# Decay in place, a one-partition gate, halved block 0, accumulated sums and a new instruction order in a linear-attention and expert kernel

## The chip, the cores and the metric

One core of one Trainium2 chip. The metric is device time of one execution in microseconds (us), as a median over several executions. A profile is one execution under the hardware profiler; its span (first to last instruction) is some 1.65 us shorter than the time of the same execution. Executions come in a fast and a slow state; ratios compare fast executions only, while medians are over all executions. All "wait" figures are idle time of an engine just before an instruction, put down to whatever released it.

## The reference

Four sequences of 768 tokens, 8 heads of 48. First a linear attention with a decaying state, then for each sequence one expert out of eight, chosen from the mean of the attention's output.

```python
for t in range(S):                                   # attention, per head
    cur = einsum('bhd,bhe->bhde', u * k_t, v_t)
    y[:, :, t] = einsum('bhd,bhde->bhe', r_t, state + cur)
    state = w * state + einsum('bhd,bhe->bhde', k_t, v_t)
x = y.transpose(0, 2, 1, 3).reshape(B, S, 384)
logits = x.mean(axis=1) @ w_gate                     # 8 experts
e_idx = argmax(logits, axis=1); gate_w = softmax(logits)[e_idx]
out[b] = gate_w[b] * (relu(x[b] @ w1[e]) @ w2[e])    # w1 384x1024, w2 1024x384
```

## The kernel before

A sequence is three blocks of 256 tokens, 12 blocks in all (block g, sequence b = g // 3). For each block k and r are scaled by powers of the decay, turned on TensorE (PE), multiplied to scores, masked on VectorE (DVE), and multiplied with v; a state in PSUM carries over. The expert's weights can only be fetched when the mean is known: gate (PE), choice (DVE), then GpSimd (POOL) reads the index and issues the transfers. The expert phase (mm1: `hp`, relu: `ht`, mm2: `op`, eviction: `ob`, store) of one sequence is interleaved with the attention of the next.

Every operation is a step with the engines that may do it; a long text gives the order. Each engine executes its steps in that order and waits for what a step needs, so an instruction that waits holds up all behind it on its engine. `b0` to `b2` are three PSUM banks that steps take and free.

```python
ORDER = """...
POOL vt 3; POOL r 5; POOL weights 0; ACT exp 0; fill 3 b0; PE at 4 0; ...
... DVE st 1 0; ...; PE carry 1; PE s 1 0; ...
SP store 1 1; SP store 1 0; SP store 1 2; ..."""

def carried(g):            # puts the decayed state back into PSUM, by a product with the identity
    nc.tensor.matmul(out=s_ps[b][:, 0 : 2 * D * NP], lhsT=ident,
                     rhs=carry[b]..., start=True, stop=False, ...)

def state_out(g, o):       # o = 1: decayed, for the next block; o = 0: within the block
    nc.vector.tensor_mul(st, s_ps[b]..., wcmask if o else bmask...)
    if o:
        carry[b] = st
        ...

def pool_mms(g):           # sums over tokens: 6 one-column matmuls for each block
    ...
def gate(b):               # logits on all 128 partitions: the stationary operand is broadcast
    for ct in range(NCT):
        nc.tensor.matmul(out=lgp, lhsT=pools[b][:, ct : ct + 1].to_broadcast([128, 128]), rhs=wg[:, ct, :], ...)

def weights(b):            # w1 as two tiles and two transfers of 384 KB, then w2
    ev = nc.gpsimd.value_load(idx8[0:1, 0:1], ...)
    for fh in range(2):
        t = wpool.tile([128, NCT, HF], BF16, tag=f"w1_{fh}", ...)
        nc.gpsimd.dma_start(out=t, in_=moe_w1[ds(ev, 1)]...[:, :, HF * fh : HF * fh + HF])
        w1s[b, fh] = t
    ...
def store(b, gi, cs):      # two transfers for one block of output
    for c in range(2):
        nc.sync.dma_start(out=dst[c][:, cs, :], in_=obs[b, gi][64 * c : 64 * c + 64, cs, :])
```

Of the kernel before, what the change touches and what calls it, by code (L numbers as in the profile page):

```python
# [19 lines left out]
DVE k 0 0; DVE r 0 0; ACT late; fill 1 b0; PE t 0 0 b0; DVE k 0 1; DVE r 0 1; J k 0; J r 0  # L20
POOL r 1; fill 2 b1; PE t 0 1 b1; ACT kr 0 1; ACT v 0; DVE kr 0 0; fill 6 b2; PE at 0 0; DVE k 1
DVE prod 0 0 b0; DVE prod 0 1 b1; DVE gt 0 0; PE t 1 0 b2; ACT kr 1 0; PE s 0 0; DVE st 0 1
PE bonus 0; PE t 1 1 b0; PE at 0 1; PE y 0 1 0; PE s 0 1; PE inter 0 1; ACT kr 1 1
DVE prod 1 0 b2; DVE gt 0 1; DVE prod 1 1 b0; POOL k 2; POOL r 2; DVE tcol 0; J vt 0; SP load 4
SP load 5; SP load 6; fill 2 b1; PE at 1 0; PE bonus 1; DVE tcol 1; DVE st 1 0; ACT v 1
POOL vt 1; DVE gt 1 0; PE t 2 1 b1; PE y 0 1 1; PE t 2 0 b2; PE carry 1; PE s 1 0; PE y 0 0 0
PE vt_y 0; PE at 1 1; DVE st 1 1; POOL k 3; POOL r 3; ACT kr 2 1; ACT kr 2 0; ACT xn 0 1
DVE gt 1 1; DVE prod 2 0 b2; DVE prod 2 1 b1; PE y 0 0 1; PE y 1 1 0; PE s 1 1; ACT xn 0 0
PE y 1 0 0; PE inter 1 0; PE at 2 0; DVE gt 2 0; PE y 1 0 1; PE inter 1 1; PE bonus 2
PE t 3 1 b0; PE at 2 1; PE turn 0 b2; DVE tcol 2; DVE st 2 0; POOL v 2; POOL vt 2; POOL k 4  # L30
POOL r 4; DVE gt 2 1; PE t 3 0 b1; PE vt_y 1; PE pool 0; PE carry 2; PE y 1 1 1; PE s 2 0
ACT v 3; ACT kr 3 1; ACT xn 1 0; ACT xn 1 1; DVE kr 3 0; DVE prod 3 1 b0; DVE st 2 1
DVE prod 3 0 b1; PE y 2 0 1; PE y 2 1 0; PE at 3 0; PE turn 1 b0; PE bonus 3; PE inter 2 1
PE y 2 0 0; PE y 2 1 1; PE vt_y 2; DVE gt 3 0; PE at 3 1; ACT v 4; ACT xt 0 b2; ACT xn 2 1
DVE tcol 3; DVE xt 1 b0; DVE gt 3 1; PE inter 2 0; ACT xn 2 0; PE t 4 1 b1; PE pool 1; PE pool 2
DVE gate_sums 0; PE t 4 0 b2; PE gate 0; ACT kr 4 1; ACT kr 4 0; DVE k 5; DVE choose 0
POOL vt 3; POOL r 5; POOL weights 0; ACT exp 0; fill 3 b0; PE at 4 0; DVE prod 4 0 b2
DVE prod 4 1 b1; DVE gt 4 0; POOL v 5; PE turn 2 b0; PE t 5 0 b2; ACT xt 2 b0; ACT kr 5 0
PE s 3 0; PE t 5 1 b1; ACT kr 5 1; DVE st 3 1; PE at 4 1; PE bonus 4; PE s 3 1; PE vt_y 3
PE inter 3 1; DVE gt 4 1; DVE st 4 0; DVE tcol 4; PE at 5 0; ACT xn 3 0; ACT xn 3 1  # L40
DVE prod 5 0 b2; DVE prod 5 1 b1; PE inter 4 0; PE carry 4; PE s 4 0; PE bonus 5
PE mm1 0 2 0 b0; PE mm1 0 3 0 b2; ACT relu 0 2 0 b0; PE mm1 0 2 1 b1; ACT relu 0 3 0 b2
ACT relu 0 2 1 b1; POOL k 6; POOL vt 4; DVE gt 5 0; DVE r 6; DVE tcol 5; PE mm1 0 0 0 b0
PE t 6 1 b2; PE t 6 0 b1; DVE st 4 1; DVE gw 0; DVE kr 6 1; DVE prod 6 1 b2; PE s 4 1; PE vt_y 4
PE at 5 1; DVE st 5 0; ACT relu 0 0 0 b0; ACT kr 6 0; DVE prod 6 0 b1; PE turn 3 b0
PE mm1 0 3 1 b2; ACT xt 3 b0; DVE xn 4 0; PE carry 5; PE mm1 0 6 0 b1; PE inter 4 1
PE mm1 0 4 0 b0; ACT relu 0 3 1 b2; DVE relu 0 6 0 b1; ACT relu 0 4 0 b0; PE inter 5 0
PE mm1 0 1 1 b2; ACT relu 0 1 1 b2; DVE gt 5 1; DVE xn 4 1; PE mm1 0 0 1 b1; PE mm1 0 5 1 b0
PE mm1 0 1 0 b2; ACT relu 0 0 1 b1; ACT relu 0 5 1 b0; PE s 5 0; DVE st 5 1; PE at 6 0
PE mm1 0 6 1 b1; DVE relu 0 1 0 b2; DVE gt 6 0; SP fence; SP load 7; SP load 8; SP load 9  # L50
PE mm1 0 7 1 b0; PE mm1 0 5 0 b2; DVE relu 0 7 1 b0; DVE r 7; ACT relu 0 6 1 b1
ACT relu 0 5 0 b2; POOL vt 5; POOL k 7; POOL r 8; PE mm1 0 4 1 b1; PE inter 5 1; PE s 5 1
PE at 6 1; PE vt_y 5; ACT v 6; ACT relu 0 4 1 b1; POOL k 9; DVE xn 5 1; PE mm1 0 7 0 b2
PE t 7 0 b0; PE pool 4; PE bonus 6; PE pool 3; PE mm2 0 5 0 b1; ACT relu 0 7 0 b2; DVE xn 5 0
DVE gt 6 1; PE pool 5; DVE gate_sums 1; PE mm2 0 5 1; DVE k 8; ACT v 7; ACT kr 7 0; PE gate 1
DVE choose 1; DVE prod 7 0 b0; PE mm2 0 1 0 b2; PE mm2 0 1 1; DVE tcol 6; ACT gated 0 5 b1
DVE vt 6; ACT gated 0 1 b2; PE t 7 1 b1; PE mm2 0 4 0 b0; PE mm2 0 4 1; PE t 8 0 b2; DVE kr 7 1
DVE prod 7 1 b1; ACT exp 1; ACT gated 0 4 b0; ACT kr 8 0; DVE r 9; PE s 6 0; PE at 7 0
PE turn 5 b1; ACT xt 5 b1; PE mm2 0 0 0 b0; PE mm2 0 0 1; DVE gt 7 0; DVE prod 8 0 b2
POOL weights 1; DVE gated 0 0 b0; PE bonus 7; PE t 9 1 b1; PE t 9 0 b2; PE t 8 1 b0; ACT v 8  # L60
ACT kr 8 1; DVE st 6 1; PE s 6 1; PE at 7 1; PE vt_y 6; ACT kr 9 0; ACT xn 6 0; DVE kr 9 1
DVE prod 9 1 b1; DVE tcol 7; DVE prod 8 1 b0; DVE st 7 0; DVE prod 9 0 b2; DVE gt 7 1; POOL vt 7
PE mm2 0 3 0 b1; PE mm2 0 2 0 b0; PE mm2 0 2 1; PE carry 7; PE inter 7 0; PE inter 6 1
PE mm2 0 3 1; PE turn 4 b2; DVE xt 4 b2; DVE gated 0 2 b0; ACT xn 6 1; PE pool 6
ACT gated 0 3 b1; PE s 7 0; PE at 8 0; DVE st 7 1; PE mm1 1 0 1 b1; PE mm1 1 5 1 b2
ACT relu 1 0 1 b1; ACT relu 1 5 1 b2; PE mm1 1 0 0 b0; ACT relu 1 0 0 b0; PE inter 7 1
PE bonus 8; PE mm1 1 6 1 b1; PE mm1 1 2 0 b2; DVE tcol 8; DVE gt 8 0; DVE gw 1
DVE relu 1 2 0 b2; DVE relu 1 6 1 b1; PE mm1 1 1 0 b0; PE s 7 1; PE vt_y 7; ACT xn 7 1
ACT relu 1 1 0 b0; ACT xn 7 0; PE at 8 1; PE mm1 1 4 0 b2; SP store 0 1; SP load 10; SP load 11
SP store 0 0; SP store 0 2; DVE st 8 0; DVE relu 1 4 0 b2; PE mm1 1 3 1 b1; DVE gt 8 1  # L70
ACT relu 1 3 1 b1; PE mm1 1 5 0 b0; ACT relu 1 5 0 b0; PE pool 7; PE inter 8 0; PE mm1 1 7 1 b2
PE mm1 1 2 1 b1; PE mm1 1 6 0 b0; ACT relu 1 6 0 b0; ACT relu 1 2 1 b1; POOL k 10; POOL vt 8
DVE r 10; POOL v 9; PE carry 8; PE s 8 0; PE at 9 0; DVE st 8 1; PE t 10 1 b0; PE inter 8 1
PE mm1 1 1 1 b1; PE s 8 1; PE vt_y 8; ACT v 10; ACT relu 1 1 1 b1; ACT relu 1 7 1 b2; DVE gt 9 0
DVE kr 10 1; DVE prod 10 1 b0; PE at 9 1; ACT xn 8 1; PE bonus 9; PE mm1 1 7 0 b1
DVE relu 1 7 0 b1; PE turn 6 b2; ACT xn 8 0; PE mm1 1 3 0 b0; PE pool 8; ACT xt 6 b2
PE mm1 1 4 1 b1; ACT relu 1 3 0 b0; ACT relu 1 4 1 b1; PE turn 8 b2; ACT xt 8 b2; POOL k 11
DVE gate_sums 2; PE gate 2; DVE gt 9 1; DVE choose 2; ACT exp 2; DVE gw 2; DVE tcol 9
PE t 10 0 b0; PE mm2 1 5 0 b1; PE mm2 1 5 1; DVE kr 10 0; DVE prod 10 0 b0; DVE vt 9
PE mm2 1 2 0 b2; PE mm2 1 2 1; DVE gated 1 5 b1; DVE gated 1 2 b2; PE at 10 0; PE s 9 0  # L80
PE mm2 1 0 0 b0; PE mm2 1 1 0 b1; PE mm2 1 1 1; ACT gated 1 1 b1; PE mm2 1 0 1; PE turn 7 b2
ACT gated 1 0 b0; ACT xt 7 b2; POOL weights 2; POOL r 11; PE t 11 0 b1; DVE gt 10 0; DVE st 9 1
PE s 9 1; PE vt_y 9; PE at 10 1; DVE kr 11 0; DVE st 10 0; PE mm1 2 3 1 b0; PE inter 9 1
DVE prod 11 0 b1; ACT xn 9 0; ACT relu 2 3 1 b0; DVE xn 9 1; PE t 11 1 b2; PE bonus 10
DVE tcol 10; PE mm1 2 0 1 b1; DVE gt 10 1; ACT relu 2 0 1 b1; PE pool 9; PE mm1 2 3 0 b0
PE inter 10 0; PE mm2 1 4 0 b1; PE mm2 1 4 1; PE carry 10; DVE relu 2 3 0 b0; ACT kr 11 1
PE at 11 0; PE s 10 0; DVE prod 11 1 b2; DVE v 11; PE mm1 2 2 1 b0; PE mm1 2 6 1 b2
ACT relu 2 6 1 b2; ACT relu 2 2 1 b0; ACT gated 1 4 b1; DVE st 10 1; DVE gt 11 0; POOL vt 10
PE bonus 11; PE s 10 1; PE vt_y 10; PE at 11 1; PE mm1 2 2 0 b2; DVE xn 10 0; ACT relu 2 2 0 b2
PE mm1 2 1 1 b0; PE mm1 2 1 0 b1; ACT relu 2 1 0 b1; ACT relu 2 1 1 b0; PE inter 10 1  # L90
DVE tcol 11; DVE st 11 0; PE mm2 1 3 0 b2; PE inter 11 0; POOL vt 11; DVE xn 10 1; DVE gt 11 1
PE mm1 2 7 0 b1; PE mm2 1 3 1; PE mm1 2 0 0 b0; PE carry 11; DVE relu 2 0 0 b0; ACT gated 1 3 b2
PE s 11 0; DVE st 11 1; PE turn 9 b2; PE mm1 2 5 0 b0; ACT relu 2 5 0 b0; ACT xt 9 b2
DVE relu 2 7 0 b1; PE s 11 1; PE vt_y 11; DVE xn 11 0; PE inter 11 1; PE mm1 2 4 0 b1
DVE xn 11 1; PE mm1 2 7 1 b0; ACT relu 2 7 1 b0; PE pool 10; PE pool 11; PE mm1 2 4 1 b2
DVE gate_sums 3; PE mm1 2 6 0 b0; PE gate 3; DVE choose 3; ACT relu 2 4 1 b2; ACT relu 2 6 0 b0
# [19 lines left out]
def kernel(  # L116
# [250 lines left out]
    def transpose_by_dma(g, i):  # L367

        if g not in krs:
            kr_tile(g)  # L370
# [173 lines left out]
    def state_out(g, o):  # L544
        b, gi = divmod(g, NB)
        if o == 1 and gi == NB - 1:
            return
# [378 lines left out]
```

## Time and profile before

| | before |
|---|---|
| time, median of 3 | 137.65 us |
| profiled execution | 141.46 us, span 139.8 |
| first expert matmul, half clock after it (us) | 38.87; 39.3 to 42.7 |
| last matmul to end of span (us) | 134.52 to 139.8 |

The slices, the windows and the chain of waits stand in the prediction. Two views are added. The first is the table of PE's waits of the kernel before (what waited and for what; total, times, longest): in the whole run there is one wait of weight.

```profile
PE hp L669 <- DMA w<-in_moe_w_dram: 2.0, 1, 2.0
PE fill L213 <- DVE zero L185: 1.3, 1, 1.3
PE twp L351 <- POOL rp L333: 0.7, 2, 0.5
```

The second is DVE's timeline of the kernel before, from the start to the choice of the first expert (start, duration, engine, line, operation, and in brackets the idle time before it).

```profile
9.05 2.57 DVE L333 TENSOR_TENSOR kp<-k,dk 128x768 bf16<-128x768 f32 x1
...
13.34 0.54 DVE L549 TENSOR_TENSOR st<-s,bmask 128x384 bf16<-128x384 f32 x1
...
28.78 0.18 DVE L607 TENSOR_REDUCE pooled<-s 128x3 f32<-128x18 f32 x1
28.87 1.03 DVE L333 TENSOR_TENSOR kp<-k,dk 128x768 bf16<-128x768 f32 x1
29.88 0.17 DVE L626 MAX8 top<-s 128x8 f32<-128x8 f32 x1
```

The first state product is out at 13.34, and the choice begins at 29.88 (MAX8). Note also the same scaling `kp`, once 2.57 us and once 1.03: the first time GpSimd was at work on its own scaling.

### The profile page before, as it was taken

What the parts mean: (1) busy time and instruction counts of PE and PEld (TensorE: products, weight loads), DVE (VectorE), ACT (ScalarE), POOL (GpSimd) and SP (SyncE); (2) the same over time, 40 slices, a digit from 0 to 9 for tenths busy, and PEclk for the clock granted to TensorE, in tenths of its full rate; (3) what the DMA queues carried; (4) which work ended last, traced back from release to release, by engine and by line L of the source; (5) the groups of instructions that cost most, each with busy time, mean ns of one, the idle gap of its engine ahead of it and who ended that gap; (6) DMA issues with size and microseconds to landing.
All of it is one profiled execution on the core that took longest, in us unless ns stands there. A gap on an engine that the chain in (4) does not pass through costs nothing.

```text
span 139.8 us, 4473 instructions
## 1 busy us (share of the span) xinstructions
PE 129.2 (92%) x1928; PEld 89.4 (64%) x1928; DVE 98.5 (70%) x193; ACT 67.6 (48%) x119; POOL 55.2 (39%) x52
## 2 busy tenths in 40 slices
PE   6998999998589999999999999999999999999940
PEld 2256677876347676778767786686767756666620
DVE  6499999996946689988659978857756336683110
ACT  0986584677235747376446483073544600422130
POOL 4158599969940537142101963804120060000000
PEclk9999999999968999999999999999999999999997
DMA  2999997979999999089649992995006559980254
GB/s 47 293 325 325 285 237 198 244 205 247 206 209 240 237 293 280 1 105 212 137 95 270 319 271 72 128 212 115 5 0 170 172 80 191 235 284 5 66 130 144
DMA packets 46473, 25.47 MB, mean 182 GB/s; under 512 B 39284, under 2 KB 45429, under 8 KB 46453
## 3 DMA queue, kind: packets, MB, share of 16 engines
q1 hardware_dynamic: 41332, 18.89, 49.9%
q0 software_dynamic: 4288, 6.29, 26.3%
q8 instruction: 15, 0.25, 0.7%
q10 hardware_dynamic: 832, 0.00, 0.3%
q14 instruction: 6, 0.04, 0.2%
HBM read 26.76 MB, written 4.72 MB: 225 GB/s over the span
## 4 chain that ended last, share of the span: by engine, by line
PE 65%; SPq 15%; DMA 10%; DVE 3%; issue 2%; POOL 1%; ACT 0%; POOLq 0%; ACTq 0%
PE op L688 23%; PE hp L669 22%; SPq L176 14%; DMA w<-in_moe_w_dram 5%; DMA r<-in_r_dram 5%; PE twp L351 4%; PE y L498 3%; PE xp L582 2%; PE at L402 2%; PE s L526 2%; PE y L468 2%; PE y L486 1%; DVE rp L333 1%; PE s L616 1%; SPq L206 1%
## 5 line engine op out<-in xcount | busy, mean ns | idle before, releaser
L669 PE MATMUL hp<-xt,w 128*128 128x384 bf16 x192 | 37.8, 338 | 2.0 <-DMA w<-in_moe_w_dram 2.0
L680 ACT ACTIVATE ht<-hp 128x384 bf16<-128x384 f32 x45 | 21.5, 490 | 34.0 <-PE hp L669 34.0
L688 PE MATMUL op<-w,ht 128*128 128x384 bf16 x192 | 34.0, 326 | 0.0
L415 DVE TENSOR_TENSOR gt<-at,mask 128x1024 bf16<-128x1024 f32 x24 | 29.2, 1217 | 1.3 <-PE at L402 1.0
L669 PEld LDWEIGHTS <-w 128*128 128x128 bf16 x192 | 20.2, 115 | 10.9 <-DMA w<-in_moe_w_dram 2.0
L688 PEld LDWEIGHTS <-ht 128*128 128x128 bf16 x192 | 18.1, 98 | 11.0 <-DVE tcol L441 0.2
L333 POOL TENSOR_TENSOR kp<-k,dk 128x768 bf16<-128x768 f32 x8 | 14.7, 1841 | 15.6 <-DMA k<-in_k_dram 15.6
L446 POOL TENSOR_TENSOR vt<-vb,tcol 128x768 bf16<-128x768 bf16 x9 | 14.0, 1551 | 16.3 <-DVE tcol L441 11.5
L339 ACT COPY kr<-twp 128x1024 bf16<-128x1024 bf16 x16 | 16.0, 1014 | 6.9 <-PE twp L351 6.9
L333 POOL TENSOR_TENSOR rp<-r,dr 128x768 bf16<-128x768 f32 x7 | 12.7, 1818 | 5.9 <-DMA r<-in_r_dram 5.8
L701 DVE TENSOR_SCALAR ob<-op,gw 128x384 f32<-128x384 f32 x13 | 7.9, 615 | 9.5 <-PE op L688 9.4
L498 PE MATMUL y<-vb,gt 64*128 64x48 bf16 x384 | 14.4, 180 | 0.2
L498 PEld LDWEIGHTS <-gt 64*128 64x128 bf16 x384 | 11.4, 93 | 3.9 <-issue 2.6
L682 DVE TENSOR_SCALAR ht<-hp 128x384 bf16<-128x384 f32 x19 | 10.2, 554 | 5.4 <-PE hp L669 5.3
L699 ACT ACTIVATE ob<-op,gw 128x384 f32<-128x384 f32 x11 | 6.4, 581 | 14.3 <-PE op L688 14.3
L654 POOL DMA_DIRECT2D w<-in_moe_w_dram x8 | 6.4, 803 | 15.7 <-DVE xt L341 9.4
L351 PE MATMUL twp<-ident,rp 128*128 128x128 bf16 x96 | 9.5, 223 | 0.8 <-POOL rp L333 0.7
L390 DVE TENSOR_TENSOR prod<-twp,kr 128x512 bf16<-128x512 bf16 x24 | 9.7, 418 | 0.7 <-ACT kr L339 0.5
L351 PE MATMUL twp<-ident,kp 128*128 128x128 bf16 x96 | 9.6, 225 | 0.6 <-DVE kp L333 0.4
L526 PE MATMUL s<-vb,kp 64*128 64x96 bf16 x160 | 10.2, 204 | 0.0
L402 PE MATMUL at<-kr 48*64 48x128 bf16 x384 | 9.9, 220 | 0.3 <-DVE gt L415 0.2
L339 ACT CAST xn<-y 128x384 bf16<-128x384 f32 x15 | 6.9, 482 | 5.1 <-PE y L486 3.5
(75 smaller groups left out, 168.6 us busy)
## 6 DMA issues: line engine op xcount, KB each, us to landing
k<-in_k_dram SPq DMA_DIRECT2D x12, 384.0 KB, 5.1
r<-in_r_dram SPq DMA_DIRECT2D x12, 384.0 KB, 6.3
v<-in_v_dram SPq DMA_DIRECT2D x12, 384.0 KB, 5.6
out_dram<-ob SPq DMA_DIRECT2D x22, 192.0 KB, 3.4
w<-in_moe_w_dram POOLq DMA_DIRECT2D x8, 384.0 KB, 6.3
w<-in_moe_w_dram POOLq DMA_DIRECT2D x4, 768.0 KB, 10.1
out_dram<-ob SPq DMA_DIRECT2D x4, 96.0 KB, 2.1
wuT<-in_w_dram ACTq DMA_DIRECT2D x2, 0.8 KB, 2.8
```

The costliest lines, as they stand in the source:

```text
L176: nc.sync.dma_start(out=t.rearrange("q h c d -> q h (c d)"), in_=src[b, :, L * gi : L * gi + L, :].rearrange("h (q c) d -> q h (c d)", c=2),)
L333: eng.tensor_mul(dst[:, cs, :, 0:D].rearrange("q c h d -> q h c d"), src[:, :, cs, :], dec[:, :, cs, :])
L339: nc.scalar.copy(dst, src)
L351: nc.tensor.transpose(out=twp[:, o + p, :], in_=src[:, c, 2 * p : 2 * p + 2, :].rearrange("s a b -> s (a b)"), identity=ident,)
L402: nc.tensor.matmul(out=at[64 * j : 64 * j + 64, a, pp, cs, :].rearrange("q (c i) -> q c i", c=2), lhsT=kt[q, p, j, cs, :], rhs=rt[q, p, j] ...
L415: nc.vector.tensor_mul(gts[g][:, rnd].rearrange("q a p c t -> q (a p) (c t)"), ats.pop((g, rnd)).rearrange("q a p c t -> q (a p) (c t)"), ...
L446: eng.tensor_mul(vts[g], vbs[g].rearrange("q c h d -> q (c h) d"), src.to_broadcast([128, 2 * H, D]))
L498: nc.tensor.matmul(out=yj[:, D * h : D * h + D], lhsT=gt[q, p // 2, a, p % 2, c, :], rhs=vb[q, c, h, :], start=begin(g, j), stop=(c == 1), ...
L526: nc.tensor.matmul(out=sp[:, 96 * p : 96 * p + 96], lhsT=kp[g % NR][qo, c, 2 * p : 2 * p + 2, :].rearrange("s a b -> s (a b)"), rhs=vb[qo, ...
L669: nc.tensor.matmul(out=hp[:, 0:SB].rearrange("q (n l) -> q n l", l=C), lhsT=w1s[b, ft // 4][:, ct, ft % 4 :: 4], rhs=xts[b][:, 3 * sb : 3 ...
L680: nc.scalar.activation(out=o, in_=src, func=ACT.Relu)
L688: nc.tensor.matmul(out=moe_ps[b, si][:, 0:DM], lhsT=hts[b][:, ft, 128 * si : 128 * si + 128], rhs=w2s[b][:, ft, :], start=(ft == 0), stop= ...
```

## The change

Five parts, and an order made anew for all of them. (1) The state decays in PSUM by a VectorE product, which needs no matmul to put it back; its copy goes to VectorE or ScalarE. (2) The gate has one weight column, so its logits lie on one partition, and a tiny matmul spreads the gate weight. (3) Block 0 is loaded, scaled and turned by halves of the heads. (4) From block 3 on, the sums over tokens are accumulator outputs of the evacuation of the turned x. (5) The last block's eviction and store are split by columns over two engines and queues, each other store is one transfer; and w1 is one tile, which from sequence 1 on comes in one transfer of 768 KB. For the single-transfer stores x is turned in token order.

```diff
-    def carried(g): ...                             # and eight "PE carry g"
+    def decay(g):
+        sp = s_ps[g // NB][:, 0 : 2 * D * NP]
+        nc.vector.tensor_mul(sp, sp, wcmask...)
     def state_out(g, o, eng=None):
+        if o: copy(eng, st, sp)
...
     def evac_x(g, eng):
+        if g in SUMS:                                # blocks 3 to 11
+            for ct in range(NCT):
+                nc.scalar.activation(out=dst, in_=xp[:, ct], func=ACT.Copy, accum_out=acc)   # or
+                nc.vector.tensor_scalar(dst, xp[:, ct], 0.0, None, op0=ALU.add, op1=ALU.add, accum_out=acc)
...
-        lgp = s_ps[b][:, TC + 2 * H : ...]
+        lgp = s_ps[b][0:1, TC + 6 * H : ...]
-                lhsT=pools[b][:, ct : ct + 1].to_broadcast([128, 128]),
+                lhsT=pools[b][:, ct : ct + 1],
+    def gate_spread(b, bank):
+        nc.tensor.matmul(out=gwp[b][:, 0:1], lhsT=one, rhs=gw1[b], start=True, stop=True)
...
-        for fh in range(2):
-            t = wpool.tile([128, NCT, HF], BF16, tag=f"w1_{fh}", ...)
+        t = wpool.tile([128, NCT, F], BF16, tag="w1", ...)
+        for f in ([slice(0, HF), slice(HF, F)] if b == 0 else [slice(0, F)]):
+            nc.gpsimd.dma_start(out=t[:, :, f], in_=src[:, :, f])
...
+    def gated_cols(si, half, eng): ...               # last block: 192 columns each on ACT and DVE
+    def store_cols(si, half, eng): ...
     def store(b, gi, cs):
-        for c in range(2): nc.sync.dma_start(...)
+        nc.sync.dma_start(out=dst[:, cs, :], in_=obs[b, gi][:, cs, :])
```

## The prediction

> **What bounds the kernel now.** I read four views, in this order. First the page's slices, to see which engine is full in which part of the run (40 slices of 3.5 us; a digit is tenths of the slice that the engine was busy; PEclk is the granted TensorE clock).
>
> ```profile
> PE   6998999998589999999999999999999999999940
> DVE  6499999996946689988659978857756336683110
> PEclk9999999999968999999999999999999999999997
> DMA  2999997979999999089649992995006559980254
> ```
>
> The reader is to see three parts. Up to about slice 10 (35 us) DVE is as full as PE, and DMA is full as well. Then slice 10 has a hole in PE, and the two slices after it a lower clock. From there to slice 38 PE is full and no other engine is. The windows view puts figures on the three parts (start:end, length, then busy us and instruction counts of PE, weight load, DVE, ACT, POOL, then clock, DMA share and rate).
>
> ```profile
> 10.00:31.00 21.00, 19.93 (x460) 15.19 (x458) 20.52 (x37) 14.28 (x20) 17.68 (x12) 1.00 0.98 252
> 31.00:38.87 7.87, 5.35 (x155) 4.04 (x153) 6.74 (x10) 3.67 (x5) 7.43 (x7) 1.00 1.10 222
> 38.87:134.55 95.68, 95.51 (x1287) 66.86 (x1287) 64.56 (x126) 43.35 (x81) 26.62 (x21) 0.98 0.71 162
> ```
>
> DVE has 20.52 of 21.00 us in the first, so the masked score evictions and their neighbours set the pace there. In the last, PE has 95.51 of 95.68: this is two thirds of the run, and a PE instruction removed there is worth its spacing, one for one. The middle part ends in the one real PE wait, which the chain that ended last shows with its cause (start, length, what):
>
> ```profile
> 23.29 6.79 DMA r<-in_r_dram
> ...
> 30.15 0.72 POOL rp L333
> ...
> 31.95 6.87 DMA w<-in_moe_w_dram
> ...
> 38.87 3.71 PE hp L669 x12
> ...
> 128.66 5.86 PE op L688 x36
> ...
> 134.59 0.58 ACT ob L699
> ```
>
> So: the r rows of block 5 land at 30.08, POOL scales them, only then does POOL's queue reach the issue of the first expert's weights, these land at 38.82, and the MoE starts. The same lines give the price of the dip in the clock: twelve matmuls in 3.71 us, where later 36 of the same width take 5.86 us (0.163 each, so 1.95 for twelve): 1.76 us lost, after a PE wait of 1.95 us.
>
> The timed runs have a median of 137.65, the profiled execution 141.46, with a span of 139.8. The difference, 3.81, is nearly that wait plus that loss (3.71). I infer, without being able to show it, that in the timed runs the weights come in time and the clock stays up.
>
> Last, the tail: the last matmul ends at 134.52, the last eviction at 135.17, then the store (two issues of 0.6 us on one queue), and the span ends at 139.8.
>
> **What the Trainium skill says.** "TensorE: Matmul & The Clock Gate", Part 1 (the HAM clock gate): a window of some 3.4 us with the array idle drops the clock to half. The trace agrees: the windows after 38.9 show clocks of 0.63, 0.50, 0.50 and 0.67 per us and 1.00 from 43. "PSUM — Partial Sum Buffer", the four PSUM rules: VectorE writes leave the written bits alone, and a matmul without the first-in-group flag adds to what VectorE left where the bit is set. That is why decay in place can do without the matmul that put the decayed state back; no run yet shows it. Same page, specifications: the forms that handle two 2-byte elements at a time are copy, tensor_tensor and tensor_scalar without an accumulator output. It is said of PSUM writes, but the trace's plain 768-element bf16 eviction at 551 ns (0.72 ns per element) fits a faster form, so I expect the accumulating one to be slower. "DMA: Bandwidth & Descriptors", SWDGE vs HWDGE vs iDMA: each DMA engine takes turns between the software and the hardware queues. The trace agrees in kind: at 34 to 35 us both move, with 67.6% and 35.9% of the engines.
>
> **The change part by part.** The instruction order was made anew for all engines, so I counted it and compared what stands before and after the first MoE matmul on PE. PE spacings are starts in the timeline between 40 and 135 us.
>
> State: the eight matmuls that copy the state back go (eight with 326 ns each, but 0.16 to 0.26 apart); five of them stand behind the first MoE matmul: about 1.1 us of PE. DVE keeps 20 state operations of 0.55 (eight decays come in, four copies go to ACT, the other four replace the old products). The chain from state to state grows by one such operation; blocks are about 8 us apart, so this is hidden except perhaps in the first 30 us.
>
> Pooling: 54 one-column matmuls (nine blocks of six) go, about 0.15 us a block, with some at 0.22: 1.5 us of PE. In exchange nine transposed evictions become three accumulating pieces each. Estimate from rows: a DVE piece 0.35 (1.05 for 0.55), an ACT piece 0.4 to 0.5 (1.4 for 0.80). Five are on DVE, four on ACT: +2.5 us DVE, about +2 ACT, in a stretch where DVE has 31 us free. Hidden, but for the gate's chain after the last block of each sequence.
>
> Gate: six passes with a 128x128 fp32 weight load (190 ns each) take 0.59 to 0.65 a sequence. With one weight column I estimate 0.25 to 0.3. Three of the four lie in the PE-bound part: -1.05. The matmul that spreads the gate weight over the partitions adds about 0.25 three times: +0.75. Its DVE copy is hidden.
>
> Order: the new one starts the MoE with less attention done: scores (0.35), state and y products (0.50), bonus (0.20) and carried-in product (0.17) of blocks 4 and 5 come after instead of before: +1.2 us in the PE-bound part. Sum for it: -1.1 - 1.5 - 1.05 + 0.75 + 1.2 = -1.7 us.
>
> Block 0 by halves: half the heads now need both halves of the decay table, so its first scaling can start at about 7.0 instead of 6.05, and DVE still does the whole k of block 1 (2.57 us) before the first mask product. I expect no gain here. But five k/r scalings at about 1.5 us leave DVE for POOL over the run; of DVE's work before the expert is chosen (30.3), a mask product (1.15), an eviction (0.6), a scaling (1.03) and an x eviction (0.5) move behind it or away, and an early bonus product (0.95) and half a state operation come in. So the choice comes about 1.5 to 2 us earlier. POOL still scales r of block 5 before it issues the weights, so most of this is not passed on; I count -0.7 us.
>
> Tail: the last eviction is split over ACT and DVE (about 0.36 against 0.58), its two stores go out on two queues at once, without the second 0.6 us issue, as 96 KB pieces (2.1 us to landing against 3.4 for 192 KB). From the last matmul, data down after about 2.7 instead of 4.0 us: -1.3.
>
> Against it: the later sequences load w1 in one transfer of 768 KB, which must be whole before their first matmul. Before, the third load was issued 1.8 us after its gate, and the second half of w1 was down 7.6 us after that. The new order has 8.4, 8.9 and 8.4 us of PE work between gate and first use (dense), against 9 to 9.4 to landing. Three waits of 0.3 to 0.7 us: +1.0, less if unprofiled DMA is faster.
>
> Sum: 137.65 - 1.7 - 0.7 - 1.3 + 1.0 = 134.95; I lean a little lower, 134.8, since larger pieces in the w1 transfer should make it quicker.
>
> **The rivals.** First, a transfer that was kept away comes back. The loads of blocks 7 to 9 stand behind a fence that needs the first gate weight. Before, DVE wrote it at 40.1, when the first w1 was down. Now it stands right after the choice on DVE, at about 32, so those loads share the engines with the first expert's weights. At the 2:1 split seen at 34 us, w1 would land some 1.8 us later: about 136.5, and more if the clock dips again. For it speaks the trace's full DMA; against it that the timed run may not wait on w1 at all.
>
> Second, the w1 waits cost the full 0.6 to 1.3 us each, so the PE savings are given back: 136 to 137. The chain before shows PE reaching the third w1 at 118.91, 1.5 us after its first half was down and 0.4 before its second half.
>
> Third, DVE becomes the bound through accumulating evictions: it would have to lose 31 us of slack; I give this little.
>
> Fourth, the early DVE-bound part shrinks by the full 2 us, because unprofiled DMA delivers r of block 5 early: about 133.
>
> **Range and chances.** The gains that need no luck (PE work, tail) are 3.0 us; the doubtful terms run from -2 to +3. That gives 132.4 to 137.3. The 2% line is 134.9, almost at my number: 0.49 faster, 0.47 within 2%, 0.04 slower.
>
> **What would show it.** Right: no one-column pooling groups after the third block, gate groups of about 0.3 us, PE over 99% busy after the MoE starts, and some 2.7 us from last matmul to last store data. Wrong: a PE wait on the weight transfer above 1 us in a later sequence; hardware-queue packets while the first w1 moves, and an MoE start after 39 us; accumulating evictions that PE waits for; a span that ends as long after the last matmul as before.

## The result, and the profile after

| | before | after |
|---|---|---|
| time, median | 137.64 us (137.24 to 137.73, 4 runs) | 150.71 us (149.39 to 152.91, 4 runs) |
| ratio of the fast runs | | 1.0923, 95% interval 1.0841 to 1.1006 |
| span of the profiled execution | 139.8 (slow) | 148.6 (fast) |

A ratio here is the mean time of one kernel's fast runs over that of the other's fast runs of the same rounds, so it is not quite the ratio of the medians. The kernel became 9% slower; 134.8 had been predicted, with 0.04 for slower.

The slices of the changed kernel, to be read as those in the prediction (40 slices of 3.7 us):

```profile
PE   6999998598879999995899999999999970999970
DVE  6285997975947969789989888886973201331330
PEclk9999999856999999999999999999999997589999
DMA  3999999997999999689996003996000999200082
```

PE now has four holes (slices counted from 0): slices 6 and 7, 10 and 11, 18 and 19, 32 and 33. After the first and the last the clock falls to half. DVE is not full at the start any more (2, 8, 5). PE's waits of the changed kernel name what the holes are:

```profile
PE hp L712 <- ACT ob L741: 4.9, 1, 4.9
PE hp L712 <- DMA w<-in_moe_w_dram: 3.2, 2, 2.0
PE y L517 <- DVE vt L486: 1.5, 1, 1.5
```

Windows of the changed kernel (length, then busy us and counts of PE, weight load, DVE, ACT, POOL; clock; DMA share; GB/s):

```profile
30.00:36.00 6.00, 5.52 (x89) 4.43 (x89) 3.38 (x12) 3.29 (x6) 4.11 (x5) 0.52 0.87 199
36.00:42.00 6.00, 4.49 (x110) 3.39 (x107) 5.52 (x12) 3.00 (x4) 5.98 (x6) 1.00 1.11 185
42.00:71.06 29.06, 27.11 (x455) 19.55 (x454) 22.31 (x51) 16.04 (x34) 20.70 (x16) 1.00 0.97 234
71.06:117.55 46.49, 46.49 (x714) 32.97 (x715) 35.88 (x86) 24.56 (x61) 12.70 (x10) 1.00 0.49 109
117.55:126.50 8.95, 4.11 (x25) 2.33 (x24) 1.36 (x3) 1.19 (x3) 0.00 (x0) 0.89 1.08 247
```

Between the holes PE is as full as it was (46.49 of 46.49). So the loss is in the holes, and I take them in turn.

**The start.** DVE's timeline of the changed kernel, the same stretch as shown of before:

```profile
14.33 0.56 DVE L575 TENSOR_TENSOR st<-s,bmask 128x384 bf16<-128x384 f32 x1 [1.44 <-PE s L549]
...
24.97 1.22 DVE L454 TENSOR_TENSOR gt<-at,mask 128x1024 bf16<-128x1024 f32 x1 [1.04 <-PE at L432]
...
26.38 2.26 DVE L486 TENSOR_TENSOR vt<-vb,tcol 128x768 bf16<-128x768 bf16 x1
...
31.98 0.16 DVE L660 MAX8 top<-s 1x8 f32<-1x8 f32 x1 [0.17 <-PE s L650]
```

The first state product is out 1.0 us later than before, after 1.44 us idle; 1.04 us idle follow at 24; then the bonus product `vt`, 0.94 us alone, takes 2.26. The choice begins 2.1 us later than before, where the prediction had it 1.5 to 2 us earlier. POOL's timeline of the changed kernel shows both sides of the slow product, and what the late choice does:

```profile
26.01 1.81 POOL L338 TENSOR_TENSOR rp<-r,dr 128x768 bf16<-128x768 f32 x1
28.05 2.26 POOL L338 TENSOR_TENSOR kp<-k,dk 128x768 bf16<-128x768 f32 x1 [0.23 <-DMA k<-in_k_dram]
30.69 1.80 POOL L338 TENSOR_TENSOR rp<-r,dr 128x768 bf16<-128x768 f32 x1 [0.38 <-DMA r<-in_r_dram]
34.01 1.70 POOL L699 DMA_DIRECT2D w<-in_moe_w_dram  x2 [1.52 <-DVE gt L454]
```

POOL's scaling ran from 26.01 to 27.82; `vt` began at 26.38 and ended 0.82 us after POOL had finished; POOL's next scaling began at 28.05, while `vt` still ran, and took 2.26 instead of 1.8. The weights are issued at 34.01, 1.6 us after the last step of the choice (32.45). So it is in all 20 profiles (1.55 to 1.57 us for sequence 0), and in none is POOL's scaling what is waited for: in that of before it ended as the issue came (31.96 and 31.95), in the gate run below 0.28 us ahead of the issue. So the choice sets the issue, and what it loses is passed on whole.

This start is not the same in each execution: with the same code up to the choice, `vt` took 2.25 us in the profile of e2 below, 2.26 in that of k1, 1.88 in that of g1 and 1.31 in that of e1, and the choice began at 31.62, 31.47, 30.95 and 30.52 (the last two profiles are of executions that count as slow). The first state product is latest in e1 (15.32), where the choice is earliest, so it is the slow `vt` that goes with a late choice, and not the late state product. That is a comparison of single executions, not an experiment.

PE waits 1.52 us for `vt` and runs at half clock from 28.9 to 35.7 by the clock records of the trace. It starts one expert matmul at 40.15, when the first half of w1 has been down for 0.5 us, and the second when the other half is down:

```profile
40.15 0.33 PE L712 MATMUL hp<-xt,w 128*128 128x384 bf16 x1
41.76 1.98 PE L712 MATMUL hp<-xt,w 128*128 128x384 bf16 x11 [1.29 <-DMA w<-in_moe_w_dram]
```

The one tile needs both halves.

**Sequence 1.** From the chain of waits of the changed kernel (start, length, what):

```profile
62.19 8.83 DMA w<-in_moe_w_dram
71.06 1.65 PE hp L712 x9
```

w1 in one transfer lands 8.83 us after its issue, 10.6 us after the gate; PE waits 1.96 us, until 71.06.

**Sequence 3.** The same chain, later:

```profile
117.55 0.63 DVE ob L743
118.22 7.56 DMA out_dram<-ob
126.53 6.88 PE hp L712 x27
```

and the ScalarE timeline of the changed kernel:

```profile
112.17 0.58 ACT L741 ACTIVATE ob<-op,gw 128x384 f32<-128x384 f32 x1 [0.81 <-PE op L730]
...
125.89 0.58 ACT L741 ACTIVATE ob<-op,gw 128x384 f32<-128x384 f32 x1 [6.47 <-DMA out_dram<-ob]
```

There are three output buffers. The last part of sequence 1's output is ready at 112.75, but its store stands behind `SP store 2 1` in the queue, whose data is ready at 118.17. Three stores leave from 118.22 on, one behind the other, while the weights of sequence 3 occupy the DMA engines; the first lands at 125.8, the next two evictions wait 6.5 us for a buffer, their PSUM banks stay taken, and PE waits 4.87 us. The clock is half from 124.5 to 131.3: 27 matmuls take 6.88 us instead of 27 x 0.1625 = 4.39.

**The end.** From the last matmul (144.13) to the end of the span it is 4.51 us instead of 5.31 (134.51 to 139.8).

### The profile page after: what moved, and what is told of

Read it like the earlier page. It is cut to its first block, busy times and chain, and to the rows that moved or that the text cites. A ratio compares the mean times of both kernels' runs of the same rounds, so it can differ in the third digit from the quotient of the medians.

```text
span 148.6 us, 4423 instructions
## 1 busy us (share of the span) xinstructions
PE 130.9 (88%) x1874; PEld 88.8 (60%) x1876; DVE 96.3 (65%) x216; ACT 71.7 (48%) x148; POOL 64.3 (43%) x58
## 4 chain that ended last, share of the span: by engine, by line
PE 56%; DMA 22%; SPq 13%; issue 2%; POOL 1%; DVE 1%; POOLq 1%; ACT 1%; ACTq 0%
PE hp L712 23%; PE op L730 16%; SPq L180 12%; DMA w<-in_moe_w_dram 10%; DMA out_dram<-ob 5%; DMA r<-in_r_dram 4%; PE y L529 3%; PE twp L363 3%; PE at L432 2%; PE xp L608 2%; DMA k<-in_k_dram 2%; PE y L507 2%; PE s L549 1%; POOL rp L338 1%; PE y L517 1%
## 5 line engine op out<-in xcount | busy, mean ns | idle before, releaser
L338 POOL TENSOR_TENSOR rp<-r,dr 128x768 bf16<-128x768 f32 x11 | 20.7, 1883 | 11.9 <-DMA r<-in_r_dram 11.9
L351 ACT COPY kr<-twp 128x1024 bf16<-128x1024 bf16 (+1 forms) x18 | 16.9, 942 | 10.6 <-PE twp L363 9.3
L741 ACT ACTIVATE ob<-op,gw 128x384 f32<-128x384 f32 x16 | 9.3, 581 | 22.8 <-PE op L730 15.8
L724 DVE TENSOR_SCALAR ht<-hp 128x384 bf16<-128x384 f32 x20 | 11.1, 556 | 13.1 <-PE hp L712 12.8
L338 POOL TENSOR_TENSOR kp<-k,dk 128x768 bf16<-128x768 f32 x10 | 18.6, 1856 | 1.2 <-DMA k<-in_k_dram 1.2
L486 POOL TENSOR_TENSOR vt<-vb,tcol 128x768 bf16<-128x768 bf16 x7 | 10.3, 1475 | 15.9 <-DVE tcol L481 15.9
L699 POOL DMA_DIRECT2D w<-in_moe_w_dram x5 | 4.1, 822 | 17.9 <-PE hp L712 10.5
L743 DVE TENSOR_SCALAR ob<-op,gw 128x384 f32<-128x384 f32 x6 | 3.7, 616 | 11.5 <-DMA out_dram<-ob 6.6
L218 PE MATMUL fill<-zero 128*128 128x512 bf16 x22 | 9.9, 539 | 1.4 <-DVE zero L189 1.3
L351 ACT CAST xn<-y 128x384 bf16<-128x384 f32 x18 | 8.2, 481 | 4.9 <-PE y L529 2.3
```

What stands on the lines that cost most here:

```text
L338: eng.tensor_mul(dst[:, cs, :, 0:D].rearrange("q c h d -> q h c d"), src[:, :, cs, :], dec[:, :, cs, :])
L351: nc.scalar.copy(dst, src)
L724: nc.vector.tensor_scalar_max(o, src, 0.0)
```

## The experiments

Theory A: the new order loses, not the operations. Theory B: the operations lose. "Changed" below is the changed kernel, "before" the kernel before; a ratio is against before's runs of the same rounds. All outputs were correct, but for the one marked. Where a run is called a gain or a loss below, it is because the interval of its ratio leaves out 1. The medians include slow executions; where that matters the median of the fast ones is given too.

### Holes of the changed kernel, one at a time

The store of sequence 1 moved to where its data is ready:

```diff
 ACT gated 1 4 b0;
+SP store 1 2;
 ... SP store 2 1;
-SP store 1 2;
```

> One store is moved in the sync queue: the store of sequence 1's last block goes ahead of a store of sequence 2 that becomes ready 5 us later. Theory 1 (a store held back in its in-order queue keeps an output buffer, and with it PE, waiting while the last weights move): the 4.87 us PE wait near 121.7 us goes and with it the half clock of 6.8 us that follows (2.5 us lost), so about 143.3 us. Rival (the buffers or the transfer rate are the limit, not the order of the stores): the wait stays or moves to another eviction, time above 148 us.

147.99 us (146.77 to 149.85; fast 147.69), ratio 1.0688 (1.0620 to 1.0757), between what the two theories expected. The wait for `ob` was gone, and only part of its 7.4 us (wait and half clock) came back. PE's waits of this run:

```profile
PE hp L712 <- DMA w<-in_moe_w_dram: 7.7, 4, 2.3
```

It waits 7.7 us for weights, four times, where the changed kernel waited 3.2 in two: behind the store's wait stood the weights' (sequence 3's w1 lands 9.07 us after its issue), with three half-clock stretches of 3.41 us.

w1 in two tiles and two transfers again, in every sequence:

```diff
-t = wpool.tile([128, NCT, F], BF16, tag="w1", ...)
+for fh in range(2): t = wpool.tile([128, NCT, HF], BF16, tag=f"w1_{fh}", ...); nc.gpsimd.dma_start(out=t, ...)
```

> The first expert matrix is again two tiles by two transfers in every sequence, as in the kernel before. Theory 2 (the one-tile form makes the first use wait for all of it): the PE waits of 1.3 us at 40.5 us and 2.0 us at 69 us go, time about 147.5 us. Rival (the transfers land at the same time however they are cut): less than 0.5 us gained.

149.31 us (148.15 to 150.18), ratio 1.0786 (1.0695 to 1.0876). Weight waits fell from 3.2 to 1.2 us, and the `ob` wait grew to 5.5. The time is 1.0 us below that of the changed kernel (fast medians), less than theory 2 had, and as the two intervals overlap it is not clear of noise.

The bonus product on POOL and the weights ahead of the scaling of r:

```diff
-DVE vt 2;                       POOL k 4; POOL r 4; POOL k 5; POOL r 5; ... POOL weights 0
+POOL k 4; POOL vt 2; POOL r 4; POOL k 5; ... DVE choose 0; POOL weights 0; POOL r 5
```

> The bonus product of block 2 goes back from DVE to POOL, between two scalings, and the weight fetch of sequence 0 goes ahead of the scaling of r of block 5. Theory 3 (the 2.26 us DVE product delays the choice of the expert, and the scaling delays the fetch): the choice ends near 31 instead of 32.4 us, the first MoE matmul starts 1.5 to 2 us earlier, the half clock from 28.7 us is shorter or gone, time about 148.5 us. Rival (POOL becomes the bound, since its work is only rearranged): the start does not move, time within 1 us of the changed kernel.

154.21 us (153.28 to 155.63), ratio 1.1203: a miss. PE waited 4.3 us in two waits for scaled r (3.4 of it for block 5), and the clock was half for 13.65 us from 28.1. POOL has no room there.

> All three edits together. If the three causes are separate and add up: 150.7 - 7.4 - 3.2 - 2 = about 138 us, that is the time of the kernel before or a little above. If the new operations themselves cost time that these waits only hide: 142 us or more.

All three together: 152.78 us (149.34 to 154.62), three of its four runs slow, so no ratio. The part that lost alone lost here too.

A fourth output buffer, which would have been the direct test of the store's wait, is not among the runs. That test is missing.

The first two alone, later:

> The changed kernel with the stalled store of sequence 1 moved ahead in its queue and w1 in two tiles, both at once; the start is left as it is. Theory C (the changed kernel's holes are stacked: each removed one hands its time to the next, and together they pay): 146 to 147.5 us, below the better single one (147.99), with the half clock of 28 to 36 us still there. Theory D (the operations lose, whatever the holes): 148 us or more.

145.47 us (143.43 to 148.15; fast 144.3, two executions), ratio 1.0455 (1.0348 to 1.0562). Expected was 146 to 147.5. By fast medians the two gain 6.0 us together, 2.6 and 1.0 alone. So the holes are stacked: each hides the next. PE's largest wait of this run is again the weights':

```profile
PE hp L711 <- DMA w<-in_moe_w_dram: 3.3, 2, 2.5
```

### Operations against order

The changed kernel's code under before's order (each new step where its predecessor stood, the spread of the gate weight at the first free bank, and the turns of x ahead of the gates that now need them):

```diff
-PE carry 1; PE s 1 0                        +DVE dec 0; DVE st 1 0; PE s 1 0
-PE pool 5; DVE gate_sums 1; ... PE turn 5   +PE turn 5 b2; ACT xt 5 b2; DVE gate_sums 1
                                             +DVE gw 1; PE gwb 1 b0; DVE gws 1 b0
```

> The changed kernel's code, unaltered, with the order of the kernel before put back: each new operation stands where its predecessor stood (decay just ahead of the state's copy, the spread of the gate weight at the first free bank after it, turns of a later sequence ahead of its gate, because the sums now come from them). Theory A, the new order loses the time (too little TensorE work between the gate and the first use of w1, the store queue, and the half clock that each hole brings): 136 to 139.5 us, of which up to 1.5 us is the wait for the whole of w1 as one tile. Theory B, the new operations or the one-tile w1 themselves lose it: 146 us or more.

162.18 us (161.95 to 163.22), ratio 1.1800. The same with w1 in two tiles:

> As the run before, with w1 in two tiles and two transfers as in the kernel before. Theory A: 135 to 138 us, at least level with the kernel before; the wait ahead of the first use of w1 in sequences 0 and 1 is 1 to 2 us shorter than with one tile. Theory B: over 145 us.

161.97 us (161.19 to 163.06), ratio 1.1761. The same with the sums by matmuls again:

> As the run before, but the pooled sums of all sequences by the small matmuls on TensorE as in the kernel before, so that the gate of sequences 1 and 3 does not wait for the evacuations of x. Theory A: within 1 us of the run before, either way: 135 to 138 us (six to nine pools of 0.15 us come back to TensorE, and the gate of sequence 1 comes 1 to 2 us earlier). If the accumulator outputs are what loses the time, it is at least 5 us faster than the run before.

146.54 us (145.96 to 147.32), ratio 1.0645 (1.0581 to 1.0710). And before's code under the changed order:

> The reverse: the code of the kernel before (carry matmul, gate on 128 columns, block 0 by columns, pools by matmul, two w1 tiles, stores in two transfers) under the order of the changed kernel. Theory A: 145 us or more, with holes at 26 to 41 us and in sequence 3 and at least two half-clock windows more than the kernel before. Theory B: 137 to 140 us.

162.61 us (160.08 to 163.00), ratio 1.1810, with a wait of 6.4 us for `ob` in sequence 3.

Theory A had 136 to 139.5 for the first two and fell; theory B had 137 to 140 for the last and fell as well. Neither the operations nor the order is the cause by itself: an order fits the durations and needs of its own operations, and each fails with the other's. PE's waits of the two-tile run under the old order show how:

```profile
PE s L650 <- DVE pooled L638: 4.5, 3, 1.6
PE gwp L682 <- DVE gw L676: 2.8, 2, 2.0
```

New edges (sum from evacuation, spread from gate weight) meet a PE queue that isn't arranged for them. These kernels are my own splices, so their size says nothing of the changed kernel's; the difference of 15 us between the second and the third is what the accumulated sums cost where the order leaves no room for them.

### The start

Two casts and scalings back on their former engines, to bring the choice forward:

```diff
-POOL v 0        +ACT v 0
-POOL k 5        +DVE k 5   (just ahead of DVE choose 0)
```

> The changed kernel with two casts and scalings of its start put back on the engine that had them before: v of block 0 on ScalarE instead of GpSimd (where it waits behind a scaling that waits for rows), and k of block 5 on VectorE ahead of the choice instead of GpSimd. Theory C (the late choice comes from VectorE standing idle 1.4 us for the first state product, then losing 1.3 us of the block 2 bonus product to GpSimd, which leaves a hole in TensorE and a half clock): the bonus product takes under 1.2 us, TensorE's wait for it is under 0.5 us, the choice is 1 to 2.5 us earlier, the expert phase starts at 39 to 40.5 instead of 41.8, and the time is 147 to 149. Rival (the state's longer chain holds the start back): the choice moves by under 0.5 us and the time stays within 0.7 us of 150.7.

153.32 us (152.58 to 153.76), ratio 1.1101: a miss. DVE's timeline of this run:

```profile
14.71 0.56 DVE L575 TENSOR_TENSOR st<-s,bmask 128x384 bf16<-128x384 f32 x1 [1.81 <-PE s L549]
...
26.86 2.26 DVE L486 TENSOR_TENSOR vt<-vb,tcol 128x768 bf16<-128x768 bf16 x1
...
32.11 0.95 DVE L338 TENSOR_TENSOR kp<-k,dk 128x768 bf16<-128x768 f32 x1
32.98 0.15 DVE L660 MAX8 top<-s 1x8 f32<-1x8 f32 x1
```

The bonus product still took 2.26: it meets the scaling of r of block 4, which I had left where it was, not that of k of block 5. The first state product was late in spite of the earlier cast, so v was not what held it. And the k that I gave to DVE stands on the way to the choice: 1.0 us later, and with it the weights' issue (35.01). With the two repairs of before:

> All three repairs at once. Theory C: 141 to 144 us, since the start's hole, the weight waits and the store wait go together and three half-clock windows with them. Theory D: 147 us or more. If it comes under 137 us the new operations gain and only their order lost.

147.26 us (145.46 to 150.97; fast 146.0), ratio 1.0576 (1.0496 to 1.0656): above the 141 to 144 expected, and no better than without the start's edit (144.3). So the start was read wrongly.

### One part alone in the kernel before

Decay in place:

```diff
-PE carry g; PE s g 0
+DVE dec g-1; DVE st g 0; ... PE s g 0
```

> The kernel before with one part of the change: the state decays in place (a VectorE product in PSUM, then a copy), no matmul that copies it back, every step where it stood. The prediction's account (eight spacings of 0.16 to 0.26 us leave TensorE, the longer chain is hidden): 136 to 137.2 us. Rival (VectorE is full until the expert is chosen, so each decay there, 0.56 us, lies on the way to the choice): the choice is 0.8 to 1.5 us later than in the kernel before, and the time is 138 to 140.

141.60 us (139.62 to 142.24; fast 139.81), ratio 1.0172 (1.0110 to 1.0234), or 2.3 us. The rival of that run holds for the time; the choice came later than it said. DVE's timeline of it:

```profile
29.45 0.17 DVE L610 TENSOR_REDUCE pooled<-s 128x3 f32<-128x18 f32 x1
29.55 2.53 DVE L333 TENSOR_TENSOR kp<-k,dk 128x768 bf16<-128x768 f32 x1
32.00 0.16 DVE L629 MAX8 top<-s 128x8 f32<-128x8 f32 x1
```

Against before (both profiles slow) the pooled sum is 0.67 us later and the choice 2.12: what DVE had more to do moved its scaling of k from a free moment into the one in which POOL began its own (29.45 to 31.26), and it took 2.53 instead of 1.03. So a delay of 0.67 became one of 2.1. The weights' issue moved from 31.95 to 34.05.

Block 0 by halves:

> The kernel before with block 0 by halves of the heads alone. The prediction's account: no gain at the start, no loss, 137 to 138 us. Rival (the two extra loads ahead put off the rows of block 1, and VectorE's scaling and GpSimd's scaling then meet): the first mask product is up to 0.9 us earlier, but the first state product is 0.7 to 1.5 us later, and the time 138 to 140.

139.54 us (138.81 to 141.33; fast 139.31), ratio 1.0114 (1.0072 to 1.0155), or 1.5 us; the edit is the change's own part 3. In the POOL timeline of this run the scaling for block 1 starts at 10.04 (before: 9.00), because the rows land later behind the two additional loads, and meets DVE's:

```profile
10.04 2.37 POOL L335 TENSOR_TENSOR rp<-r,dr 128x768 bf16<-128x768 f32 x1 [3.20 <-DMA r<-in_r_dram]
```

The first mask product is 0.87 us earlier (11.34), but the state product comes 0.49 later than before (13.83) and the choice 0.77 later (30.65). This is the late state product of the changed kernel, where the scaling starts at 10.07 and takes 2.34.

The gate on one partition:

> The kernel before with the gate on one partition alone; the spread of the gate weight stands between two halves of an expert output product whose neighbour bank is free, the gate weight of sequence 3 is computed earlier. The prediction's account: four gates of 0.62 become four of 0.3, three or four spreads of 0.25 to 0.3 come in: 137 to 137.8 us. Rival (each spread is a new place where TensorE stands behind VectorE's queue, as in the run with the old order, where four spreads cost 3.1 us): waits at the spread of 1 us or more in all, 138 to 140 us.

140.08 us (139.73 to 140.72), ratio 1.0166 (1.0125 to 1.0206), or 2.1 us. PE's timeline of this run:

```profile
52.48 0.29 PE L617 MATMUL s<-wg,pooled 128*1 128x8 f32 x6
52.71 0.82 PE L702 MATMUL op<-w,ht 128*128 128x384 bf16 x4
53.73 0.38 PE L650 MATMUL gwp<-gw,one 1*128 1x1 f32 x2 [0.20 <-DVE prod L391]
...
95.01 0.38 PE L650 MATMUL gwp<-gw,one 1*128 1x1 f32 x2
95.64 1.14 PE L683 MATMUL hp<-xt,w 128*128 128x384 bf16 x6 [0.25 <-DVE gw L655]
```

The gate itself takes 0.23 us of PE (start to start) instead of 0.65. The spread takes 0.31 and in my places more, since it borrows one of three banks from the flow around it: against steps that both kernels have, the run falls back 1.07 us around the spread at 95.01. The idle times at the spreads add up to 0.45 us only, where the rival had 1 us or more, so most of the loss isn't in a wait that the profile names. A gate that is cheaper by 0.4 is worth less than a spread that is badly placed.

The changed tail, first with rows permuted (its output layout needs x in token order; this run is the one with a wrong result, and does the same work):

> The kernel before with only the changed tail: last block of sequence 3 by column halves on two engines and two queues, one transfer for each store. The prediction counted 1.3 us for it; the changed kernel's trace shows 0.84, because the second half waits for the first. So 136.5 to 137.2 us if nothing else moves, 0.8 to 1 below the kernel before. Rival: one 384 KB store on one issue lands later than two of 192 KB and holds the ob buffers, and the time stays at 137.6 or rises.

137.27 us (136.80 to 139.62), ratio 0.9933 (0.9884 to 0.9982). Then with right rows:

> The kernel before with the changed tail alone, x in token order so that the rows come out right. If the tail gives what the earlier run with permuted rows showed: 136.5 to 137.2 us, 0.5 to 0.9 below the kernel before, and faster than both kernels. If x in token order costs something at its evacuation: 137.4 us or more.

136.97 us (136.70 to 137.50, 6 runs), ratio 0.9936 (0.9898 to 0.9974). This is the one part that gains alone, 0.9 us, and the fastest kernel. The tail with the gate:

> The kernel before with the changed tail (rows now right: x in token order, one transfer for each store) and the gate on one partition. If both parts keep what they give alone: the tail's 0.9 us and the gate's 0 to 0.8, so 136 to 137 us, below both kernels. If it lies above 137.6 the two do not add.

139.23 us (139.10 to 139.60), ratio 1.0107: the two add, the gate's loss included.

The wrong-rows run also settles a guess of the prediction. Its start is that of before, and in the fast state PE's timeline reads:

```profile
37.06 2.14 PE L670 MATMUL hp<-xt,w 128*128 128x384 bf16 x12 [0.56 <-DMA w<-in_moe_w_dram]
```

A wait of 0.56 instead of 1.95, and twelve matmuls in 2.14 without a dip.

Last, the accumulated sums in the order made for them, taken back alone:

```diff
-SUMS = range(3, N)
+SUMS = ()                       # and "PE pool g" ahead of "PE turn g", g = 3 to 11
```

> The changed kernel, in its own order, with only the pooled sums taken back to small matmuls on TensorE (six for each of nine blocks, just ahead of the block's turn). The prediction's account: 1.4 us of TensorE come back, so 151.5 to 152.5. Rival (the accumulating evacuations, 1.05 and 1.7 us for a block in place of 0.55 and 0.8, hold back the gate and the matmuls behind them, as they did under the old order, where they cost 15 us): 149.5 us or less.

152.44 us (150.68 to 155.59), ratio 1.0970 (1.0910 to 1.1030), against 1.0923 (1.0841 to 1.1006) of the changed kernel in other rounds. The fast medians differ by 1.2 us (151.5 and 150.29), in the sense of the prediction (1.4); the intervals overlap, so the gain is likely and not shown. The rival, that the sums hold the changed kernel back, falls.

## Why the prediction was wrong

The span grew by 12.6 us against a fast run of before (136.0). Put together from the traces, start to end:

```
first full expert matmul at 41.76 instead of 37.06             +4.70
  weights issued 2.16 later (34.01, 31.85 in the gate run)
  first half lands 5.60 after its issue, not 5.13;
  the second half, needed too, 2.10 later
wait for w1 in sequence 1                                      +1.96
wait for the output buffer in sequence 3                       +4.87
half clock after it (6.88 - 4.39)                              +2.49
end, from the last matmul                                      -0.80
rest, by difference (TensorE's work, and what isn't named)      -0.62
                                                       sum     12.6
```

- **"So the choice comes about 1.5 to 2 us earlier"** is the step that failed at the start: it came 2.1 later. I had counted the work that leaves DVE and left out what it waits for. The decay's longer chain was called hidden "except perhaps in the first 30 us"; alone in before it puts the choice off by 2.1 us. Block 0 was called neutral; alone it puts the choice off by 0.77. These two shares are shown for before's order; that they are also the reason in the changed order rests on the same lines being late there (state product, `vt`), and was not shown by repairing it there, since two such attempts lost. The prediction also had POOL's scaling of r between the choice and the issue, "so most of this is not passed on". The issue follows the choice by some 1.56 us in each profile, so a late choice is passed on whole; whether POOL would have held back an early one no run shows. And "DVE keeps 20 state operations" is a miscount: the traces have 20 before and 24 after (12 products, 8 decays, 4 copies).
- **"Three waits of 0.3 to 0.7 us"** for w1: the mechanism was right, the size was not. 1.3 us in sequence 0 and 1.96 in sequence 1, where w1 was down 10.6 us after the gate instead of 9 to 9.4 (the larger piece, 8.83 us from issue, was not quicker); that of sequence 3 lay behind a longer wait, and came to light (2.46 us) when that one was taken away.
- **The sum had no term for the output buffers.** Three stores behind each other on one queue, the first not ready until 118.17, three buffers: this is in the order's text, and I did not follow it. With the half clock it is 7.4 us, the largest single loss. Removing it returned 2.6 us alone and 6.0 with the weights' repair.
- **Half clock.** Each hole was priced at its own length. Half clock followed two of them here, 6.8 us each time. The prediction cites the Trainium skill for a window of 3.4 us with the array idle and says that the trace agrees; in that trace PE was idle for 1.95 us only, so what agrees is the half clock and its length, not the idle window.
- **PE work:** -1.7 predicted, about -0.6 by difference. In it the gate was right: in the changed trace 0.23 and 0.31 (start to start), so 3 x (0.23 - 0.65) + 3 x 0.31 = -0.33, where -0.30 was predicted. The sums' -1.5 is likely, the matmuls moved behind the start were not measured apart. That accumulating evictions are slower was right: 1.11 us for a block on DVE instead of 0.55, 1.2 on ACT instead of 0.80.
- **Tail:** -0.80 instead of -1.3. The halves don't run side by side: the VectorE half starts when the ScalarE half has ended (143.76 after 143.30 + 0.42). The Trainium skill, "PSUM — Partial Sum Buffer", PSUM bank collisions raise a hardware error, says that two engines on one bank must not meet, reads included, and that a compiler serialises them; the trace agrees with the latter.
- **The fence rival** did not happen: the loads that it frees were issued from 37.2 on and hardly moved while the weights did: from 36.0 to 41.7 the hardware queue had 1.8% of the engines' time.
- **The range:** sure gains of 3.0 with doubtful terms from -2 to +3 make 132.65 to 137.65, not 132.4 to 137.3.
- **Right:** that the timed runs of before have neither the wait nor the dip (wait 0.56, start 37.06 in a fast run); that PE is full between the holes.

What stays open: how the 6.3 us that are left with the stores and weights repaired (144.3 against 138.0 of before in the same rounds, fast) divide between the start, the waits that came up behind the repaired ones and the half clocks; what a fourth output buffer would give; and whether an order exists in which decay in place pays.

## What to carry to other kernels

An order for engines that execute in sequence is tuned to durations that hold only in it; count a change in such a kernel not by the work that it removes but by following, for each engine, who waits for the first use of each new result, and for each queue, what stands behind an entry that isn't ready. On an engine that is full ahead of a decision (here DVE ahead of the choice), half a microsecond more can become two when it moves one operation into the time of another engine's. Change the parts one by one: here the smallest, the tail, was worth 0.9 us, and the three others tried alone (decay, block 0, gate) cost 1.1 to 1.7%; the accumulated sums and the one-tile w1 were not tried alone in the kernel before.

## What the Trainium skill lacked or had wrong

- "GPSIMD Engine Reference", section 1 (Specifications), says that the SBUF interfaces are shared with VectorE and that instructions with two SBUF inputs contend. That section gives no size. The runs agree and give one: a VectorE product of 0.94 to 1.03 us took 2.26 to 2.57 when a GpSimd product of 1.81 was under way, and ended 0.8 us after it; GpSimd's took 2.26 to 2.54 when VectorE's was.
- "TensorE: Matmul & The Clock Gate", Part 1, has the clock fall after an idle window of about 3.4 us. Here stretches of 3.41 or 6.83 us at half clock followed waits of 1.24 us (decay alone) and 1.52 us (changed kernel, at 28.7), while one of 1.96 us (changed kernel, at 71.06) was followed by none. So a hole well below a window can cost one, and its length alone does not tell.
- "DMA: Bandwidth & Descriptors", SWDGE vs HWDGE vs iDMA, tells of turns between the queues, not of what a store behind a running weight transfer pays: 7.56 us to landing for the first of three, where a store of the same 384 KB with little else under way took 2.82 (changed kernel, 141.30). From 117 to 127 us the software queue had 80.4% of the engines' time and the hardware queue 27.4%.
- No page that I found gives the time from a choice on VectorE to GpSimd's issue of a transfer by the chosen index: 1.55 to 1.57 us for the first sequence in all 20 profiles (in the changed kernel 32.45 to 34.01), and 1.24 for sequence 3 of the changed kernel (112.88 to 114.12).
